# Where a recurrent attention kernel puts one filler unit: ahead of the output rounds or behind them

## The chip, the cores and the metric

The kernel runs on one core of a Trainium2 chip. The metric is device time in microseconds (us) of one execution, the median of several runs. Every duration below comes from one profiled execution of the kernel or from those runs.

## The reference, cut to what matters

Two blocks follow each other on 2048 rows of 640 features. The first is an attention over segments of 32 rows with a memory of 8 rows, and each segment's memory is the output of the segment before. The second is a feed-forward block with a squared ReLU. Both have a layer norm in front and a residual behind.

```
mem = mem0
for s in range(n_seg):                        # 64 segments of 32 rows, one after the other
    xs = x[:, s * seg_len:(s + 1) * seg_len, :]
    h = concatenate([mem, xs], axis=1)        # 8 + 32 rows of 640
    q, k, v = h @ Wq, h @ Wk, h @ Wv          # 32 heads of 128 each
    p = softmax(mask(q @ k.T * scale))
    o = (p @ v) @ Wo
    mem = o[:, :M, :]                         # what the next segment starts from
    outs.append(o[:, M:, :])
...
h = x + attention(layernorm(x));  h2 = h + w2(relu(w1(layernorm(h)) + b1)**2) + b2
```

So segment s+1 can't begin its projections before the first 8 output rows of segment s are there.

## The kernel before, in words

**Blocks and segments.** 2048 rows are 16 blocks `b` of 128 rows, and each block is four segments, called places `sp` = 0 to 3 here. `step(b, sp)` (line 459) issues all work of one segment; it is called 64 times in order. A segment is written (b,sp) below.

**Rows.** A segment has 8 memory rows and 32 token rows. The memory rows and the first 24 token rows go through TensorE together as a tile of 32 (`hT4`, named `hT` in the profile). The last 8 token rows of four segments are put together in a tile of 32 for a whole block (`hTt`, or `ht` where the tile lies elsewhere): the tails. Tails depend on no memory, so their projections can be computed at any time before their block starts. They are the filler.

**Matmuls in groups of four.** All projections and the output rounds use 32 columns of the weight side, and four matmuls stand side by side on the four strips of 32 columns of the array. Each matmul is issued with a weight load of its own.

**The order of a segment on TensorE**, as it is written in `step`:

1. query and key projections of both halves of the heads (`project`, lines 471 to 488: 20 matmuls of 512 columns each; some are split in two of 256 by `align`, see below), with the memory rows' scores of the first half (`scores(0)`) in front of the last one's evacuation;
2. value projection of the first half (line 569 and 584), the token rows' scores, the value projection of the second half (lines 590, 600 and 605), between them `scores(1)` and `values(0)`, which multiplies the first half's memory softmax by the values. VectorE copies its result from PSUM to `oT` (line 255, through `values_out`);
3. one filler unit, if the list is long enough (line 607: the line that is changed);
4. the output rounds 0 to 5 (`wo_rounds`, line 619: four matmuls of 320 columns each; they read the `oT` of line 255), the token rows' values of the segment before (`token_values`, 40 small matmuls), `values(1)`, whose result ScalarE copies to `oT` (line 257), rounds 6 and 7;
5. one filler unit (line 626);
6. rounds 8 to 15 (lines 627 and 630; they read the `oT` of line 257);
7. all that is left of the filler (line 666).

**From the last round to the next segment.** `mem_to_hT` (lines 291 to 300): VectorE turns the rounds' sums (line 297), ScalarE copies half of them (line 298), VectorE adds them into the next segment's `hT` (line 300). The next segment's query projection reads that. In front of line 297 VectorE has the sum over the token softmax (line 635), in order. Behind line 298 ScalarE has the copy of `wo_out` (line 287), and behind that the evacuations of filler tiles (lines 264 and 266).

**The filler lists.** `fill` is filled in the loop over blocks and places and taken from its front:

```python
864  elif b < NB - 1:
865      if sp == 0:
866          fill += tail_units(b + 1, "q")[0:DC] + tail_quarters(b + 1, "q", 1, 0)
867      if sp == 1:
868          parts = tail_units(b + 1, "k")
869          fill += tail_quarters(b + 1, "q", 1, 1) + parts[0:DC]
870      if sp == 2:
871          fill += parts[DC:]
872          if quarters:
873              fill += tail_quarters(*quarters.pop(0))
874  if sp == 3 and b > 0:
875      fill += wo_tail_units(b - 1)
```

`tail_units` gives five entries of four matmuls of 512 columns; `tail_quarters` gives three entries of eight, eight and four matmuls of 256 columns, that is two and a half units of work. Together they are eight entries, or 7.5 units. `wo_tail_units` gives ten entries (one or two output rounds of a tail block each). In block 0 the lists have 31, 10, 10 and 8 entries. `quarters` has one set for (0,3) and for place 2 of blocks 1 to 13; (14,2) has five entries and block 15 none in places 0 to 2. `run(fill, 100)` at the end of each step empties the list. The first entry of a set takes a PSUM buffer from a ring of three (`mmtile`), the last one evacuates it by ScalarE to a row tile, from which VectorE turns it into place later (`late`) or, for values, SP stores it to memory.

**align.** The kernel keeps a count of the instructions on TensorE (`issued`, two for each matmul and its weight load) and splits projection matmuls in two, so that a border of a block of 256 instructions stands 34 instructions behind the start of the token scores of the first half, in every segment (`BLOCK`, `AHEAD`, `PLACE`, lines 112 and 122).

The function that the change touches, with what calls it:

Of the kernel before, what the change touches and what calls it, by code (L numbers as in the profile page):

```python
# [16 lines left out]
def kernel(  # L17
# [284 lines left out]
    fill, late, mid, owed = [], [], [], [[], [], []]  # L302

    def run(q, n):
        while n > 0 and q:
            q.pop(0)()
            n -= 1
# [151 lines left out]
    def step(b, sp, v=None):  # L459
        s = b * 4 + sp  # L460
        last = s == NS - 1
# [142 lines left out]
        if not ready:  # L604
            proj(wv, "half", lhs, 1, ps1, 3, DC)
            nc.scalar.copy(out=v[:, 512:1024], in_=ps1[:])  # L606
        if not last and len(fill) > 7:
            run(fill, 1)
        if not last:
            pT1 = soft2(1)  # L610
# [231 lines left out]
    for b in range(NB):  # L842
        for sp in range(4):
# [47 lines left out]
            if 2 <= e <= NK4 + 1:  # L891
                late.append(lambda e=e: prep_stats0(e - 2))
                mid.append(lambda e=e: prep_norm0(e - 2))
            step(b, sp, v0 if b + sp == 0 else None)

    def end_output(s):
# [118 lines left out]
```

## Time and profile before

| | |
|---|---|
| median of 3 runs | 956.94 us (956.52 to 958.64) |
| the profiled execution's own time | 958.06 us |
| its span, from the first to the last instruction of the program | 956.3 us |
| TensorE busy with matmuls | 929.1 us, 25874 matmuls |
| VectorE, ScalarE, GpSimd busy | 699.7, 548.4, 258.2 us |
| one segment, blocks 2 to 14, places 0 / 1 / 2, query start to query start | about 11.9 / 11.96 / 11.92 us |

How the lines are read. PE is TensorE's matmuls, PEld its weight loads, DVE VectorE, ACT ScalarE, POOL GpSimd, SP the engine that issues most DMAs. A timeline line gives the start in us from the span's start, the length, engine, line of the kernel, operation, the tiles written and read, the shape and the count of instructions merged in it; in square brackets stands how long the engine was idle ahead of it, and which instruction ended that. All matmuls go through one helper and so have line 116; they are told apart by their tiles: `ps<-wv,hT` is a value projection, `ps<-wq,hTt` a filler unit, `pw<-wo,oT` an output round. Ends of matmuls are modelled by the profiler; starts are measured.

### The profile page before, as it was taken

How to read it: one execution, taken by the hardware profiler on the slowest of the kernel's cores; microseconds unless marked ns; L12 is line 12 of the kernel's file. 1: busy time of each engine (PE TensorE's matmuls, PEld its weight loads, DVE VectorE, ACT ScalarE, POOL GpSimd, SP SyncE). 2: the span in 40 equal slices, each digit the busy share in tenths (PEclk: the TensorE clock that was granted, in tenths of full speed). 3: DMA queues.
4: the chain of work that ended last, by engine and by line, in shares of the span. 5: the costliest groups of instructions: out<-in, count | busy, mean ns of one | idle time of the engine just before them, and what ended most of it. 6: DMA issues, size and time to landing. Idle time of an engine off the chain costs nothing.

```text
span 956.3 us, 57547 instructions
## 1 busy us (share of the span) xinstructions
PE 929.1 (97%) x25874; PEld 570.3 (60%) x25883; DVE 699.7 (73%) x2136; ACT 548.4 (57%) x1343; POOL 258.2 (27%) x798
## 2 busy tenths in 40 slices
PE   4989999999999999999999999999999998999998
PEld 2545666666666666666666666656666665555555
DVE  3167778888888888888887787878787888566532
ACT  2556666666666666666666666656666665523321
POOL 1013222222222222222222222222222233263300
PEclk9999999999999999999999999999999999999999
DMA  9973210101010101010101010101010111643320
GB/s 360 396 235 90 45 29 13 29 13 30 10 33 9 34 10 34 9 34 9 33 10 34 9 32 11 32 11 32 11 32 11 53 43 21 199 113 86 94 56 28
DMA packets 60838, 56.74 MB, mean 59 GB/s; under 512 B 27696, under 2 KB 56752, under 8 KB 58672
## 3 DMA queue, kind: packets, MB, share of 16 engines
q1 hardware_dynamic: 59712, 52.73, 18.3%
q8 instruction: 202, 3.31, 1.5%
q10 hardware_dynamic: 880, 0.34, 0.1%
q14 instruction: 44, 0.36, 0.1%
HBM read 38.37 MB, written 9.44 MB: 50 GB/s over the span
## 4 chain that ended last, share of the span: by engine, by line
PE 93%; DMA 3%; DVE 2%; ACT 1%; issue 1%; ACTq 0%; DVEq 0%
PE ps L116 63%; PE pw L116 16%; PE y L116 6%; PE po L116 5%; DMA vt_d<-row 2%; PE sm L116 1%; PE pa L116 1%; DMA om<-in_A_mem_dram 1%; ACT otc L298 0%; ACTq L157 0%; ACT row L266 0%; DVE otr L297 0%; DVE kTt L269 0%; DVE qT L269 0%; DVE kT L269 0%
## 5 line engine op out<-in xcount | busy, mean ns | idle before, releaser
L116 PEld LDWEIGHTS <-hT 128*32 128x32 bf16 x8383 | 216.9, 96 | 146.2 <-DVE hT L300 20.7
L116 PE MATMUL pw<-wo,oT 128*32 128x320 bf16 x4224 | 178.4, 300 | 0.2
L116 PE MATMUL ps<-wv,hT 128*32 128x512 bf16 x2520 | 177.5, 380 | 0.0
L116 PE MATMUL ps<-wq,hT 128*32 128x512 bf16 (+1 forms) x3168 | 160.6, 336 | 4.8 <-DVE hT L300 4.8
L116 PE MATMUL ps<-wk,hT 128*32 128x512 bf16 (+1 forms) x2575 | 159.7, 375 | 0.0
L641 POOL TENSOR_TENSOR pkt<-ek,rk 128x64 bf16<-128x64 bf16 x64 | 19.3, 301 | 421.7 <-DVE rk L639 408.4
L116 PEld LDWEIGHTS <-oT 128*32 128x32 bf16 x4224 | 100.9, 96 | 44.8 <-ACT oT L257 9.1
L269 DVE STREAM_TRANSPOSE qT<-row 128x512 bf16<-128x512 bf16 x128 | 89.5, 699 | 24.4 <-ACT row L264 20.5
L264 ACT ACTIVATE row<-ps 128x512 bf16<-128x512 f32 (+1 forms) x170 | 93.7, 562 | 13.7 <-PE ps L116 11.7
L937 ACT ACTIVATE wv<-ps,b1f 128x512 bf16<-128x512 f32 (+1 forms) x56 | 37.6, 673 | 66.5 <-PE ps L116 66.0
L442 ACT CAST oT<-po 128x512 bf16<-128x512 f32 x128 | 74.7, 586 | 0.0
L298 ACT COPY otc<-otr 64x40 f32<-64x40 f32 x126 | 28.2, 224 | 71.5 <-DVE otr L297 71.1
L453 POOL COPY qz<-qT 128x96 bf16<-128x96 bf16 x126 | 33.5, 266 | 112.5 <-DVE mx L503 58.2
L116 PEld LDWEIGHTS <-hTt 128*32 128x32 bf16 x1640 | 45.1, 97 | 31.4 <-issue 2.0
L266 ACT CAST row<-ps 128x512 bf16<-128x512 f32 (+1 forms) x113 | 61.6, 560 | 1.9 <-PE ps L116 0.5
L635 DVE TENSOR_REDUCE zk<-ek 128x8 f32<-128x320 bf16 x64 | 31.1, 486 | 42.9 <-ACT ek L633 42.9
L116 PEld LDWEIGHTS <-v 32*128 32x128 bf16 x4064 | 42.1, 91 | 32.8 <-issue 18.4
L116 PE MATMUL y<-wq,wk 128*128 128x320 bf16 x448 | 61.2, 299 | 0.2 <-DVE wk L938 0.2
L484 ACT CAST row<-ps 128x256 bf16<-128x256 f32 x126 | 40.8, 376 | 30.3 <-PE ps L116 30.2
L257 ACT CAST oT<-po 128x128 bf16<-128x128 f32 x63 | 16.8, 267 | 65.3 <-PE po L116 65.3
L606 ACT CAST v<-ps 128x512 bf16<-128x512 f32 x63 | 37.0, 587 | 29.7 <-PE ps L116 29.7
L116 PEld LDWEIGHTS <-qz 128*32 128x32 bf16 x2016 | 36.0, 95 | 28.1 <-ACT em L506 1.9
(109 smaller groups left out, 1659.9 us busy)
## 6 DMA issues: line engine op xcount, KB each, us to landing
wv<-in_A_Wv_dram SPq DMA_DIRECT2D x5, 1024.0 KB
wq<-in_A_Wq_dram SPq DMA_DIRECT2D x5, 1024.0 KB
wk<-in_A_Wk_dram SPq DMA_DIRECT2D x5, 1024.0 KB
vt<-vt_d SPq DMA_DIRECT2D x60, 64.0 KB
xt<-in_A_x_dram SPq DMA_DIRECT2D x18, 160.0 KB
wo<-in_A_Wo_dram SPq DMA_DIRECT2D x2, 1280.0 KB
wo<-in_A_Wo_dram SPq DMA_DIRECT2D x4, 640.0 KB
wq<-in_B_w_dram SPq DMA_DIRECT2D x1, 2080.0 KB
```

The source lines that it names most:

```text
L116: nc.tensor.matmul(*a, **k)
L264: nc.scalar.mul(out=row, in_=ps, mul=scale)
L266: nc.scalar.copy(out=row, in_=ps)
L269: nc.vector.transpose(out=dst[:, n * 16:(n + 1) * 16, 0:32], in_=row.rearrange("p (h e) -> p h e", e=32))
L298: nc.scalar.copy(out=tc_[:, a], in_=tr[64:128, a, :, 0:M])
L442: nc.scalar.copy(out=oTg[:, n, :, :, M:NK], in_=po[:, :, n * 128:(n + 1) * 128].rearrange("p g (j q) -> p g j q", q=32))
L453: nc.gpsimd.tensor_copy(out=d.rearrange("p a (j f) -> p a j f", j=3)[:, :, :, 0:M], in_=src[:, :, 0:3, :])
L484: nc.scalar.copy(out=row[:, u * 256:(u + 1) * 256], in_=ps[:, u * 256:(u + 1) * 256])
L606: nc.scalar.copy(out=v[:, 512:1024], in_=ps1[:])
L635: nc.vector.tensor_reduce(out=zk[:], in_=ek[:], op=ALU.add, axis=AX.X)
L641: nc.gpsimd.tensor_tensor(out=pkt[:], in0=ek[:, :, SEG:NK], in1=rk[:].unsqueeze(2).to_broadcast([128, HG, TL]), op=ALU.mult)
L937: nc.scalar.activation(out=r[:, 0:w], in_=ps[:, 0:w], func=ACT.Relu, bias=b1f[:, fc:fc + 1], scale=1.0)
```

## The change

One number: the list has to have more than eight entries, where it had to have more than seven, for a unit to be run ahead of the output rounds.

```diff
         if not ready:
             proj(wv, "half", lhs, 1, ps1, 3, DC)
             nc.scalar.copy(out=v[:, 512:1024], in_=ps1[:])
-        if not last and len(fill) > 7:
+        if not last and len(fill) > 8:
             run(fill, 1)
         if not last:
             pT1 = soft2(1)
```

With a list of eight entries nothing is run at this point now; the unit behind round 7 is the first of the list, where it was the second, and seven entries follow the last round, where six did. Lists of ten or more entries are run as before, and so are lists of five and none. No instruction is added or dropped.

## The prediction

> **What bounds the kernel now.** I read the page first: TensorE is busy 97% of the span, the chain that ended last lies 93% on it, and the clock row is full throughout.
>
> ```profile
> PE 929.1 (97%) x25874; PEld 570.3 (60%) x25883; DVE 699.7 (73%) x2136; ACT 548.4 (57%) x1343; POOL 258.2 (27%) x798
> ...
> PEclk9999999999999999999999999999999999999999
> ...
> PE 93%; DMA 3%; DVE 2%; ACT 1%; issue 1%; ACTq 0%; DVEq 0%
> ```
>
> So a unit that is only moved changes nothing by its own work; what counts is how much of TensorE's few idle hundredths it covers in its old place and in its new one. The view of waits names two that bear on it: the weight load's waits for `hT` of line 300 (the next segment's input, 20.7 us over the kernel) and for `oT` of line 255 (the output rounds' input, 7.7 us). A weight load can wait while the matmuls ahead of it still run, so I do not use these totals. I go by the starts of matmuls. Four matmuls on the four column strips start within 0.01 us and count as one group; undisturbed, the next group starts 0.2155 us later behind one 512 wide, 0.1357 behind one 320 wide, 0.109 behind one 256 wide (starts in the trace of segment (2,0), block 2, place 0). What is beyond these is idle.
>
> Front of segment (2,0), TensorE's matmuls and weight loads in the timeline:
>
> ```profile
> 156.82 0.62 PE L116 MATMUL ps<-wv,hT 128*32 128x512 bf16 x8
> 157.26 0.39 PE L116 MATMUL ps<-wq,hTt 128*32 128x512 bf16 x4
> 157.48 0.31 PE L116 MATMUL pw<-wo,oT 128*32 128x320 bf16 x4
> ```
> ```profile
> 157.31 0.28 PEld L116 LDWEIGHTS <-oT 128*32 128x32 bf16 x8 [0.16 <-DVE oT L255]
> ```
>
> The middle row of the first fence is the unit that the change moves. The rounds' weights could be loaded at 157.31, but the unit's group runs to 157.48. From the first value matmul to the first round is 0.66 us. Segment (14,2) has only five entries in its list and so already goes without a unit there:
>
> ```profile
> 760.48 0.61 PE L116 MATMUL ps<-wv,hT 128*32 128x512 bf16 x8
> 760.97 0.32 PE L116 MATMUL pw<-wo,oT 128*32 128x320 bf16 x4
> ```
>
> There it is 0.49 us. It is the row for what the change makes of the front. Segments (15,0) to (15,2) give the same interval within 0.003 us.
>
> End of segment (2,0), matmuls, then VectorE, then ScalarE:
>
> ```profile
> 160.55 1.37 PE L116 MATMUL ps<-wq,hTt 128*32 128x512 bf16 x32
> 161.90 1.27 PE L116 MATMUL ps<-wq,hT 128*32 128x512 bf16 x26
> 163.03 0.40 PE L116 MATMUL ps<-wk,hT 128*32 128x512 bf16 x4
> ```
> ```profile
> 160.78 0.58 DVE L297 STREAM_TRANSPOSE otr<-pw 128x160 f32<-128x160 f32 x2 [0.24 <-PE pw L116]
> 161.42 0.42 DVE L300 TENSOR_TENSOR hT<-otr,otc 64x40 bf16<-64x40 f32 x2
> ```
> ```profile
> 162.38 1.44 ACT L264 ACTIVATE row<-ps 128x512 bf16<-128x512 f32 x3
> ```
>
> The 32 fill matmuls are 3 groups of 0.2155 and 5 of 0.109: 1.19 us, done at 161.75. The next segment starts at 161.90, 0.05 us after line 300 ends. TensorE idles 0.152 us. The last round to this start is 1.470 us, in all 42 segments within 0.005.
>
> **The change part by part.** A list of exactly eight entries stands in 42 segments: places 0 and 1 of blocks 1 to 14, place 2 of blocks 1 to 13, and (0,3). The trace shows a unit in front of the rounds in just these and in the segments with ten entries or more, which keep it. The moved unit is four matmuls 512 wide (in place 1 eight 256 wide, 0.218 us), their weight loads and one PSUM buffer; it issues no DMA and no copy, so SP's and POOL's queues keep their order. The slot behind round 8 gets the first unit in place of the second, of the same size in all four kinds. Behind the last round stand seven entries in place of six.
>
> *Front, removed: 0.2155 (0.218) of work.* Added: the wait for line 255 is now bare. By (14,2) it leaves 0.050 us idle, and the group behind a wait takes 0.010 longer. The last value group to the last round goes from 3.372 to 3.214 us: everything behind it comes 0.158 earlier. What could be late next is VectorE's reduction (line 635) ahead of line 297. In (2,0) it ended 0.24 us before line 297 started; in (14,2):
>
> ```profile
> 763.71 0.49 DVE L635 TENSOR_REDUCE zk<-ek 128x8 f32<-128x320 bf16 x1 [0.60 <-ACT ek L633]
> 764.28 0.58 DVE L297 STREAM_TRANSPOSE otr<-pw 128x160 f32<-128x160 f32 x2
> ```
>
> It still ends 0.08 us early, and the last round to line 300's end takes 1.416 us, as in (2,0) (1.415). So `hT` comes the full 0.158 earlier.
>
> *End, added: 0.2155 (0.218) of work.* It first fills the 0.152 (0.157 in place 1) of idle time; the fill then outlasts `hT` by about 0.065, so the next segment waits for nothing, as in (0,1) and (0,2), where long fills already give no gap. The first group behind the wait took 0.227, undisturbed 0.2155: 0.0115 saved.
>
> *Behind it, the first key matmuls.* They start at 163.03, 0.037 us late: they take the PSUM buffer that the first of ScalarE's three copies above frees (162.38 to 162.98), and that copy comes behind line 287, which comes behind line 300. The copies move 0.158 earlier, the matmuls 0.09 to 0.14: this gap closes too, with 0.02 us to spare. It stands behind place 0 (0.037) and place 2 (0.020), not behind place 1, where the buffer's copy comes earlier.
>
> Net gain of one segment: end idle + slow group + key gap - front (0.060). Place 0: 0.152 + 0.0115 + 0.037 - 0.060 = 0.140. Place 1: 0.157 + 0.0115 - 0.060 = 0.108. Place 2: 0.152 + 0.0115 + 0.020 - 0.060 = 0.123. (0,3): 0.10.
>
> Exceptions: in (9,0) and (13,0) a pause within the fill left only 0.047 and 0.084 of end idle: 0.035 and 0.07. In (1,1) the reduction ran right up to line 297, so `hT` can't come earlier: 0. Sum: 12 x 0.140 + 13 x 0.108 + 13 x 0.123 + 0.10 + 0.035 + 0.07 = 4.9 us.
>
> *One charge against it.* `align` keeps books on TensorE's instructions in blocks of 256 and puts one border just behind the first token scores. The next border is then counted out as 16 matmuls into `token_values` (12 in place 1); the trace has six unexplained pauses there among 62 segments, at just these matmuls, of 0.05 to 0.25 us; (3,1) has one of 0.16 behind matmul 12. Without the front unit TensorE reaches this border, now behind matmul 20, about 0.13 earlier. If such a pause ends at a fixed time, each grows by that. No row shows this for the changed order in bulk; the bounds are nothing (none of the four segments without a unit pauses there) and some 0.25 per segment (the longest seen). I am near the first: five of the six fall in changed segments ((0,3), (1,1), (3,1), (9,2), (14,1)), so 5 x 0.13 = 0.65 at most; as each pause may also end earlier, I take 0.4 us. The Trainium skill, "Runtime: NRT & Kernel Launch", section "Instruction fetch mechanics", says instructions arrive in blocks of 256 fetched ahead, and that crossing a border is "mostly hidden"; by it alone this charge is nothing and the sum stays 4.9. The trace agrees with the block and with mostly: six pauses in 62.
>
> Sum: 4.9 - 0.4 = 4.5 us. The span of the profiled execution would go from 956.3 to 951.8; it lay 1.8 us under that execution's own 958.06 and 0.6 under the median 956.94. From the median: 952.4.
>
> **The rivals.** *The reduction holds `hT`* (within 0.2%). If line 635 ended 0.08 us later in the changed segments, line 297 could not start earlier, and the whole front gain would end as a wait for `hT`, as in (1,1). The segment then starts when it did before: 956.9. For it: VectorE is 73% busy, and its chain does not move with the rounds. Against: relative to the value matmuls line 635 ends at 3.48 us in 61 segments of 62.
>
> *The border pauses every time* (slower). The place is `token_values`, the price up to 0.25 us per segment. From (4.9 + 1.9) / 42 = 0.16 us a segment on, the kernel is slower by over 0.2%; at 0.16, the pause of (3,1), it is 956.9 - 4.9 + 6.7 = 958.7, and at the longest 962.5. For it: the pauses exist and TensorE now comes earlier. Against: place 3 of blocks 1 to 14, whose front unit is 0.08 shorter, pauses in one segment of 14, the four without a unit in none.
>
> *It doesn't do what it says*: another number of segments would change, if lists carried entries over. `run(fill, 100)` empties them in every step, so 42 stands; with none the time is 956.9.
>
> **How the numbers follow.** Forecast 0.80 (951 to 955.2, its gain between 1.7 and 6), the reduction 0.09, the border 0.06, no effect 0.02, more than forecast 0.03. Predicted 952.4. The range 951.0 to 955.2 leaves out the other cases, some 0.2. The 0.2% that a measurement of this kernel can tell from no change is 1.9 us: faster 0.83, same 0.11, slower 0.06.
>
> **What would show it.** In (2,0) after: the first round 0.49 us behind the pair of value groups; nine groups of fill (36 matmuls) behind the last round; no wait for `hT` in front of the next segment; the first key group of the next segment 1.08 us behind its query start (1.13 before); the whole segment about 0.13 shorter. The total of waits for `hT` by the weight load falls from 20.7 to some 10 us, that for `oT` grows. I am wrong if the weight load for `hT` still waits in most places 0 to 2, if pauses of over 0.1 us stand in `token_values` in many segments, or if ScalarE's copy moves less than the matmuls and the key gap stays.

## The result

The changed kernel takes 953.58 us (median of 6, 951.63 to 954.06), beside 957.59 us (956.52 to 958.82) for the kernel before in the same comparison: a ratio of 0.9950, 95% interval 0.9936 to 0.9963, that is 3.5 to 6.1 us less. The ratio is the comparison's own estimate; the two medians alone lie 4.0 us apart, a ratio of 0.9958. The forecast of 952.4 from 956.94 is a ratio of 0.9953. The profiled execution's span went from 956.3 to 952.2 us.

The view of waits of TensorE's weight loads, in the changed kernel (us in total, times, longest):

```profile
PEld L116 <- issue: 36.2, 115, 1.7
PEld L116 <- DVE oT L255: 19.6, 62, 0.4
...
PEld L116 <- DVE hT L300: 11.2, 20, 1.5
```

The two waits that the forecast named have changed places: that for `oT` rose from 7.7 to 19.6 us, that for `hT` fell from 20.7 to 11.2. The sums are nearly equal, and the kernel is still faster, because a weight load that waits is not yet an idle TensorE: ahead of the rounds most of its wait lies beside the last value group.

Segment (2,0) in the changed kernel. The timeline's matmuls at the front:

```profile
155.67 0.61 PE L116 MATMUL ps<-wv,hT 128*32 128x512 bf16 x8
156.16 0.32 PE L116 MATMUL pw<-wo,oT 128*32 128x320 bf16 x4
```

From the pair of value groups to the first round is 0.49 us, where it was 0.66. At the end, matmuls, then VectorE, then ScalarE:

```profile
159.25 1.58 PE L116 MATMUL ps<-wq,hTt 128*32 128x512 bf16 x36
160.65 1.25 PE L116 MATMUL ps<-wq,hT 128*32 128x512 bf16 x26
161.74 0.82 PE L116 MATMUL ps<-wk,hT 128*32 128x512 bf16 x12
```
```profile
158.90 0.49 DVE L635 TENSOR_REDUCE zk<-ek 128x8 f32<-128x320 bf16 x1 [0.60 <-ACT ek L633]
159.47 0.58 DVE L297 STREAM_TRANSPOSE otr<-pw 128x160 f32<-128x160 f32 x2
160.11 0.42 DVE L300 TENSOR_TENSOR hT<-otr,otc 64x40 bf16<-64x40 f32 x2
```
```profile
161.07 1.49 ACT L264 ACTIVATE row<-ps 128x512 bf16<-128x512 f32 x3
```

36 fill matmuls stand behind the last round. They are 4 groups of 0.2155 and 5 of 0.109 us, 1.41 in all, and 159.25 + 1.41 is 160.66: the next segment's query matmuls follow without a gap. Line 300 ends at 160.53, so `hT` is there first. The key group comes 1.085 us behind the query start (1.131 before).

The shortest length of a segment in blocks 2 to 13, query start to query start. The shortest one has none of the chance pauses that the experiment on borders below is about:

| place | before | after | difference | second profiles, before / after |
|---|---|---|---|---|
| 0 | 11.899 | 11.807 | -0.092 | 11.899 / 11.806 |
| 1 | 11.955 | 11.811 | -0.144 | 11.957 / 11.810 |
| 2 | 11.918 | 11.818 | -0.100 | 11.918 / 11.815 |
| 3 | 12.327 | 12.290 | -0.037 | 12.325 / 12.293 |

The sum over the four places is 0.373 us a block; the forecast's three terms, 0.140 + 0.108 + 0.123, make 0.371. They are spread otherwise here, since a slow first group and a key gap are paid in the segment behind the one that makes them.

### The profile page after: what moved, and what is told of

It reads as the page before. It is cut to its first block, busy times and chain, and to the rows that moved or that the text cites. A ratio compares the mean times of both kernels' runs of the same rounds, so it can differ in the third digit from the quotient of the medians.

```text
span 952.2 us, 57555 instructions
## 1 busy us (share of the span) xinstructions
PE 923.5 (97%) x25883; PEld 571.5 (60%) x25883; DVE 702.1 (74%) x2136; ACT 547.5 (57%) x1343; POOL 256.4 (27%) x798
## 4 chain that ended last, share of the span: by engine, by line
PE 92%; DMA 5%; DVE 2%; ACT 1%; issue 1%; ACTq 0%; SPq 0%; DVEq 0%
PE ps L116 63%; PE pw L116 16%; PE y L116 6%; PE po L116 5%; DMA wk<-in_A_Wk_dram 2%; PE sm L116 1%; DMA wq<-in_A_Wq_dram 1%; DMA ht<-in_A_x_dram 1%; DMA om<-in_A_mem_dram 1%; DVE wk L938 0%; ACT otc L298 0%; DVE lnst L173 0%; DVE otr L297 0%; DVE kTt L269 0%; DVE hT L300 0%
## 5 line engine op out<-in xcount | busy, mean ns | idle before, releaser
L116 PEld LDWEIGHTS <-hT 128*32 128x32 bf16 x8383 | 221.3, 96 | 134.6 <-DVE hT L300 11.2
L116 PEld LDWEIGHTS <-oT 128*32 128x32 bf16 x4224 | 97.1, 96 | 54.1 <-DVE oT L255 19.6
L116 PEld LDWEIGHTS <-wk 128*128 128x128 bf16 x448 | 40.5, 98 | 20.8 <-issue 5.0
```

The lines of the kernel that those rows point to most:

```text
L116: nc.tensor.matmul(*a, **k)
```

## The experiments

Each is built on the changed kernel. "Theory" is the forecast's: a unit costs on TensorE what no wait covers at its place.

**No unit in front, in any segment.**

```diff
-        if not last and len(fill) > 8:
+        if not last and ready and len(fill) > 8:
```

> No unit in front of the rounds in any segment from (0,1) on: place 3 of blocks 1 to 14 and (0,1), (0,2), which kept theirs, lose it too. Theory (a unit costs what no wait covers, and behind the last round these long fills already outlast hT by some 0.4 us): in place 3 the rounds start 0.087 earlier, the slot behind round 7 (now 0.136 of work against a wait of 0.225) stands idle for 0.09, 0.271 of work comes behind the last round, nothing of it covered: 0.16 us lost per segment, 14 segments; (0,1) and (0,2) lose 0.06 each; together some 2.3 us slower than the changed kernel, 1.9 to 2.5 us faster than the kernel before. Rival one (the earlier start of the rounds is the gain, a unit behind the rounds is free anywhere): 16 x 0.08 = 1.3 us faster than the changed kernel. Rival two (the place of a unit does not matter, the change gained by other instruction borders): no change in place 3's length of 12.29.

Measured: ratio to the kernel before 0.9970 (0.9960 to 0.9981), 953.48 against 956.42 us. The changed kernel's 0.9950 gives 1.9 us more than that; the intervals overlap, so the trace decides. Segment (2,3), matmuls in the timeline, first in the changed kernel:

```profile
194.81 2.06 PE L116 MATMUL ps<-wo,oTt 128*32 128x320 bf16 x52
196.69 0.40 PE L116 MATMUL ps<-wq,hT 128*32 128x512 bf16 x4
```

and in this one:

```profile
195.95 2.21 PE L116 MATMUL ps<-wo,oTt 128*32 128x320 bf16 x60
197.99 0.39 PE L116 MATMUL ps<-wq,hT 128*32 128x512 bf16 x4
```

Eight more matmuls stand behind the last round, and the query starts 2.04 us behind the first of them in place of 1.88 (in the changed kernel with a pause of 0.11 within it, so 1.77 without). The first round does come 0.087 earlier. Place 3 lasts 12.446 us (median) where 12.290 is its pause-free length: 0.156 lost, against an expected 0.16. (0,1) and (0,2) lose 0.06 and 0.055. So rival one falls: behind the rounds a unit is free only as far as the wait for `hT` reaches. Rival two, no change, falls too.

**The slot's unit behind the rounds as well.**

```diff
-        run(fill, DC if ready else 1)
+        if ready or len(fill) != 8:
+            run(fill, DC if ready else 1)
```

> In the 42 lists of eight the unit behind round 7 goes behind the last round as well. Theory: that slot is a wait for line 257 of 0.225 us (segments without filler show it), so it covers the whole unit; taking it away brings round 8 no earlier and adds 0.2155 behind the last round, where nothing covers it any more: 42 x 0.22 = 9.1 us slower than the changed kernel, about 0.5% slower than the kernel before. Rival one (units behind the last round are free, as the moved one was): no change against the changed kernel. Rival two (place does not matter): no change.

Measured: ratio 1.0047 (1.0030 to 1.0063), 960.7 against 956.42 us. Against the changed kernel's ratio that is 9.3 us of loss, where 9.1 were expected. Matmuls and then one weight load of (2,0) in the timeline:

```profile
158.24 1.78 PE L116 MATMUL pw<-wo,oT 128*32 128x320 bf16 x40
159.84 1.80 PE L116 MATMUL ps<-wq,hTt 128*32 128x512 bf16 x40
161.47 0.50 PE L116 MATMUL ps<-wq,hT 128*32 128x512 bf16 x8
```
```profile
158.74 0.94 PEld L116 LDWEIGHTS <-oT 128*32 128x32 bf16 x32 [0.39 <-ACT oT L257]
```

Rounds 6 to 15 come out as one line, but within it round 8 still waits for line 257, and they last as long as with the unit between them: the last value group to the last round is 3.215 us in both kernels. All 40 fill matmuls stand at the end, and the query starts 1.751 us behind the last round in place of 1.535. The same move of the same kind of unit gains at one place and loses at the other.

**One unit left out.**

```diff
         o = wo_out(pw)
+        if eight:
+            fill.pop(0)
         run(fill, 100)
```

`eight` is `not ready and len(fill) == 8`, taken just ahead of the front slot (its line is not shown).

> Leaves out part of the computation: in each of the 42 lists of eight the second entry (one fifth of a tail projection's contraction, four matmuls of 512 or eight of 256 columns) is not computed, so that six entries follow the last round again, with nothing in front. Theory: hT is ready only 0.064 us before the fill ends, so of the 0.2155 us left out only 0.064 shows, less 0.0115 for the slow group behind a wait, and in place 0 the key matmuls then wait for ScalarE's copy: the query start comes 1.471 us behind the last round in place of 1.535, with a wait for line 300 again, and the whole kernel is 1.5 to 2.3 us faster than the changed one. Rival (after the change the end is plain TensorE work and hT is far from it): 42 x 0.2155 = 9.1 us faster than the changed kernel, query start 1.32 behind the last round.

Measured: ratio 0.9936 (0.9921 to 0.9951), 950.26 against 956.42 us: 1.3 us less than the changed kernel by the ratios, where 9.1 us of matmuls were dropped. That is a little under the 1.5 to 2.3 expected. In the trace the shortest lengths of the four places sum to 0.10 us less a block, some 1.4 us over 14 blocks. Matmuls and weight loads of (2,0):

```profile
159.20 1.37 PE L116 MATMUL ps<-wq,hTt 128*32 128x512 bf16 x32
160.54 1.27 PE L116 MATMUL ps<-wq,hT 128*32 128x512 bf16 x30
161.67 0.40 PE L116 MATMUL ps<-wk,hT 128*32 128x512 bf16 x4
```
```profile
160.54 0.98 PEld L116 LDWEIGHTS <-hT 128*32 128x32 bf16 x31 [0.26 <-DVE hT L300]
```

The wait for line 300 is back, the query start lies 1.469 us behind the last round (expected 1.471), and the key gap of some 0.03 us is back in 21 segments. So after the change the end of a segment stands 0.064 us from being bound by `hT` again.

**VectorE later.**

```diff
+        for _ in range(2):
+            nc.vector.reciprocal(out=rk2[:], in_=zk[:])
         if not last:
             mem_to_hT(pw, ...)
```

> The changed kernel with two more VectorE instructions (reciprocals of 128 x 8 to a tile of their own that nothing reads) between line 635 and line 297 of every segment. Estimate from the row of line 639 (0.20 us alone): 0.3 to 0.4 us more on VectorE there. Theory: line 635 ends 0.09 us before line 297 may start and hT stands 0.064 ahead of the fill's end, so about 0.15 of it is hidden in the 42 segments and the rest, 0.15 to 0.25, comes back as a wait for line 300: 6 to 11 us slower than the changed kernel; place 3 (0.20 and 0.42 in hand) loses nothing. Rival (with the wait for hT gone, VectorE's chain has room): no change against the changed kernel.

Measured: ratio 1.0056 (1.0037 to 1.0075), 963.99 against 959.44 us: 10 us more than the changed kernel, at the upper end of 6 to 11. VectorE and the weight loads of (2,0) (from line 635 on, line numbers of this kernel are one to three higher; the line that allocates `rk2` is not shown above):

```profile
160.26 0.48 DVE L636 TENSOR_REDUCE zk<-ek 128x8 f32<-128x320 bf16 x1 [0.60 <-ACT ek L633]
160.78 0.44 DVE L638 RECIPROCAL rk<-zk 128x8 f32<-128x8 f32 x2
161.14 0.53 DVE L297 STREAM_TRANSPOSE otr<-pw 128x160 f32<-128x160 f32 x2
```
```profile
162.21 0.34 PEld L116 LDWEIGHTS <-hT 128*32 128x32 bf16 x12 [0.30 <-DVE hT L300]
```

`hT` comes 0.26 us later behind the last round (1.67 for 1.415) and the query 0.19 later (1.724 to 1.727 for 1.535): 0.064 of the delay is hidden, the rest is paid. The key gap is back as well: the key group comes 1.130 us behind the query start in place 1, as in the kernel before. In place 3 the query start stays at 1.892 where no pause falls. The rival in the forecast that lets line 635 hold `hT` is therefore a real mechanism; it did not happen in the changed kernel, where in (2,0) line 635 ends at 159.39 and line 297 starts at 159.47.

**Place 1 alone.**

```diff
-        if not last and len(fill) > 8:
+        if not last and len(fill) > (8 if sp == 1 else 7):
```

> Only place 1 of blocks 1 to 14 is changed; places 0 and 2 and (0,3) keep the unit in front. Theory (the gain is local, and its terms lie in the segment and just behind it): place 1 gains 0.108 each, some 1.5 us against the kernel before and 3.3 us less than the full change; idle of 0.15 at the end of places 0 and 2 and the key gaps behind them (0.037, 0.020) stay as before. Rival (the gain comes from chaining, each segment's earlier start being what lets the next gain): place 1 alone gains clearly under 0.1 each, under 0.7 us in all.

Measured: ratio 0.9990 (0.9981 to 1.0000), 955.41 against 956.42 us, 1.0 us less. The interval ends at no change and holds both 1.5 and 0.7, so the times don't tell the two apart. The trace does: front 0.256 us and query start 1.533 us in place 1, just as in the full change, and 0.422 and 1.470 in places 0 and 2, just as before. By the median lengths place 1 is 0.100 us shorter than before, place 2 behind it 0.011, and place 0 is 0.002 longer: 0.109 a block, where the theory had 0.108. Place 1 needs no change in its neighbours. Only behind (1,1) the query start lies 0.035 us later than in the other segments of place 1; the point on the reduction below takes this up.

**Borders 16 instructions later.**

```diff
-    BLOCK, AHEAD, PLACE = 256, 65, 34
+    BLOCK, AHEAD, PLACE = 256, 65, 50
```

> The changed kernel with PLACE 50 in place of 34, so every border of 256 instructions stands 16 instructions (8 matmuls) later in each segment. Theory (the chance pauses in token_values are instruction borders, not data): pauses of over 0.05 us there stand behind matmul 28 in place of 20, in some three to eight segments, none of them behind 20; those in place 3's tail rounds move two groups later; the time stays within 2 us of the changed kernel. Rival (they are waits for data, line 660's or the values of the segment before): they stay behind matmul 20.

Measured: 953.18 us in one run. Twelve segments pause in `token_values`, more than expected: six of them behind matmul 28 (0.19 to 0.99 us), two behind matmul 24 (0.10 and 0.19, both in segments that kept a front unit), none behind 20. In place 3's tail rounds the pauses come 11.89 us behind the query start, most of them, in place of 11.61, two groups of 0.136 later. So the pauses that moved go with the borders of the instruction blocks, as the kernel counts them, and not with the data that the matmuls there read. Four small ones (0.06 to 0.15 us, behind matmuls 17 and 19) fit neither count and stay unexplained.

**Tail rounds of block 14 earlier.** The traces showed three segments with much uncovered waiting, (15,0) to (15,2), so I tried to use one.

```diff
-            if sp == 3 and b > 0:
+            if sp == (3 if b < NB - 1 else 1) and b > 0:
                 fill += wo_tail_units(b - 1)
```

> The changed kernel, with the ten tail-round entries of block 14 run in (15,1), which has no filler and waits 1.34 us for hT behind the last round, 0.22 in the slot and 0.05 in front, in place of (15,3), where 64 matmuls of 320 columns (16 groups of 0.136, 2.2 us) are all on TensorE's way. Theory: (15,3) is 2.2 us shorter, (15,1) about 0.55 longer (12.33 in place of 11.79, as place 3 elsewhere): 1.6 us faster than the changed kernel, 0.66% faster than the kernel before. Rival (the last segment's work is hidden, since the feed-forward weights or the last softmax end later): (15,1) 0.55 longer and nothing shorter, 0.5 us slower than the changed kernel.

Measured: ratio 0.9953 (0.9937 to 0.9968), no gain over the changed kernel that can be measured. (15,1) became 12.320 us long, as expected (12.33). But from the query start of (15,3) to the first feed-forward matmul the time fell only from 14.48 to 13.60 us, 0.9 in place of 2.2. The waits of the weight loads and of the matmuls in the last segment and just behind it, in this kernel:

```profile
PEld L116 <- ACT oT L442: 1.5, 1, 1.5
```
```profile
PE pw L116 <- DVE pTt L655: 1.2, 1, 1.2
```

Neither wait stands there in the changed kernel. The tail rounds in (15,3) were cover for the last tokens' softmax and their copy to `oT`: a wait the theory had not priced. The rival is half right.

**Second profiles of both kernels**, unchanged, to see what is chance.

> The kernel before, a second profile, to see what is chance. Theory: end idle, front and key gaps of the regular segments the same to 0.005 us; the pauses in token_values (0.75 us in six segments in the first profile) fall on other segments and sum to anything between 0.2 and 1.3 us. If the change made these pauses longer (the charge of 0.4 us in the forecast), both profiles of the kernel before lie under the changed kernel's.

> The changed kernel, a second profile. Theory: regular segments of 11.81 us in places 0 to 2, no wait for hT; the 0.72 us wait in (0,3) of the first profile is gone, since it was a chance pause of VectorE; pauses in token_values sum to between 0.2 and 1.3 us, no more than in the kernel before. If the charge was right, they sum to some 0.4 us more than in the kernel before.

Measured: 955.54 and 951.61 us. The regular lengths agree with the first profiles within 0.003 us (table above). From the query start behind (0,0) to that behind (15,2) the first pair went from 749.19 to 745.33 us, the second from 747.14 to 742.24: 3.9 and 4.9 us. The difference is pauses. In the first profile of the changed kernel (0,3) waited 0.72 us for `hT`, as VectorE started line 300 only 0.60 us after line 298, which it reads, had ended, and so stood idle for 0.85 us; no other profile has that.

## Why the prediction was right, point by point

- **What bounds the kernel**: shown. Moving equal work changed the time by what it covered: 4 us less in front of `hT`, 9 us more out of the slot.
- **The front** (0.050 idle and 0.010 for the group behind the wait, everything 0.158 earlier): measured 0.044 to 0.052 idle in all 42 segments; last value group to last round 3.215 for 3.372, so 0.157.
- **The end** (0.152 covered, `hT` first by about 0.065): the query start lies 1.535 us behind the last round (1.532 in place 1), and `hT`'s weights are loaded 0.062 to 0.070 ahead of it in 41 of the 42 segments; the other is (0,3) with the 0.72 above.
- **The key gap** closed with its 0.02 to spare: no key gap above 0.016 us is left, where 26 were.
- **The reduction** did not hold `hT`. In (1,1) the forecast gave no gain since line 635 had run up to line 297; in the changed kernel it ended 0.082 us early there, as elsewhere. The error is 0.1 us. But that lateness does not look like chance. It stands in all three profiles in which (0,3) and (1,0) keep their front unit (both of the kernel before, and place 1 alone), where line 635 of (1,1) ends 0.28 to 0.29 us later against the values than in other segments, and in none of the eight other profiles. In these three ScalarE starts line 633 there 0.37 to 0.38 us after line 615 ends, in the changed kernel 0.09; why is open. In place 1 alone the reduction did hold `hT` in (1,1): line 297 started 0.083 us before line 635's end, `hT` came 1.512 us behind the last round in place of 1.414, and the query start 0.035 later. So 0.28 us of lateness cost `hT` 0.10, and 0.18 of it was covered. The forecast's price for this rival was too high: line 635 ending 0.08 us later would not have taken the gain.
- **The sum** of 4.9 us without the charge: 4.9 between the second profiles, 3.9 between the first.
- **The charge of 0.4 us** for borders is not settled. Pauses of over 0.04 us in `token_values` sum to 0.80 and 0.28 us in two profiles with the front unit, and to 0.69 to 1.21, mean 0.93, in the seven profiles without it and with the border at its old place (both of the changed kernel, and those of the first four experiments above and of the tail rounds). The mean difference is 0.4, as charged, but two profiles of the kernel before are few for something that varies this much, and place 1 alone, with the unit gone from 14 of the 42, has 0.19. The time can't tell 4.5 from 4.9 either: its interval, 3.5 to 6.1, holds both. That pauses would grow because TensorE comes earlier was not tested by itself. As far as this term goes, it is luck that the total fits so well. What is shown is that the border rival did not decide: in those seven profiles 3 to 7 segments pause, not 42.
- **The time** from the median: 952.4 was forecast from 956.94. The kernel before has a median of 957.59 once three more runs are counted, and the changed one 953.58, so the level is 1.2 us off; the ratio agrees to 0.0003.

## What to carry to other kernels

Price filler by what each slot still has uncovered, to the hundredth: here the slots of one segment had 0.05, 0.225 and 0.15 us, and the same unit of 0.22 us was worth moving out of the first, not out of the second, and only into the third. Segments that already run without the thing a change removes are the best rows for a forecast; four such segments gave this one the price of a front without the unit, 0.060 us, which all the others were set against. And look beyond the wait you remove for the next one in line: the gain here ended 0.065 us from the old wait, and the VectorE chain in front of it had some 0.18 us to spare, as the late line 635 in (1,1) showed.

## What the runs showed of the hardware

A border of 256 instructions on TensorE, as the kernel counts them, mostly costs nothing and now and then a pause of 0.05 to 0.5 us, once 0.99; in `token_values` 1 to 12 of 62 segments had a pause, and with the borders 16 instructions later 8 of 12 pauses stood 8 matmuls later. Some places pause often: (1,0) in six of the eleven profiles, (11,3) in five. A group of four matmuls behind a bare wait takes 0.010 to 0.012 us longer than one in a stream (0.227 for 0.2155 at 512 columns, 0.146 for 0.136 at 320). Between VectorE's end of line 255 or 300 and the weight load that waits for it lie 0.051 to 0.058 us in the 42 segments of both profiles of the changed kernel.
